# The opening of a two-layer convolution and GEGLU kernel: order of its first stage, filter tiles by sums and differences, and pair additions on GpSimd

## The chip, the core and the metric

The kernel runs on one core of a Trainium2 chip. The metric is the device time of one execution in microseconds (us). The core has a matrix engine (TensorE, PE in the profile; its weight loads are PEld), a vector engine (VectorE, DVE), a scalar engine (ScalarE, ACT), a general engine (GpSimd, POOL) and a queue engine (SyncE, SP). Each works through its own list of instructions in order. Matrix results land in PSUM, which GpSimd does not read here; everything else lies in SBUF.

## The reference

With S = 2048 tokens and D = 576 channels, four steps are applied to x = A_q:

```
x = x + A(layernorm(x));  x = x + B(layernorm(x));  x = x + A(layernorm(x));  x = x + B(layernorm(x))

A(q): kv = (k * shift_k summed over 4 taps along the sequence) * v
      y  = causal long convolution of kv with ssm_k over the sequence (by FFT) + kv * ssm_D
      return q * y
B(x): (gelu(x @ w_gate) * (x @ w_up)) @ w_down        w_gate, w_up: 576 x 4608
```

k, v and the filters do not depend on x, so y is computed once for both layers. Inputs and output are 16-bit.

## The kernel before

The sequence is cut into four chunks of 512 tokens, and a chunk into four row tiles of 128 partitions (`RT`). The convolution of a chunk is a short discrete transform by matrix products with cosine and sine tables (`W`, `Wx`): the filter chunk gives four frequency tiles `h0[kt]`, the kv chunk gives `kc[kt]`, each with a cosine and a sine part (s = 0, 1) of 576 columns. Their complex products (`kacc`, which calls `prod`, L365: a product of 1152 elements and an addition of 576, twice) go through the inverse tables into four output tiles Y0 to Y3 of the chunk.

Most of the run is the feed-forward part: gate/up matmuls (`gu`, L1570 for the first unit, L1650 later) and down matmuls (`dn`, L1684). A planner (`fill`, with the model times `t.pe`, `t.dve`, `t.act` and the costs `C_...`) threads the convolution of the later chunks between them. `quarter` (L247) makes such work units for the planner.

The change lies in the opening, which comes before the first gate/up matmul and whose order is written out by hand in `begin` (L833). The steps it issues are:

- The taps of the first kv chunk. The tap weights reach the partitions by small matmuls (L891, L899), and ScalarE copies them to `sx` (L901). The first 384 channels go through TensorE with diagonal matrices `dg` (L896) and transposed k (`kT`, `shift_taps`, L820); the last 192 channels go through VectorE (`taps_rest`, L945 to L953). Products with v end both (`taps_v`, L943; L953). Meanwhile GpSimd copies the tap weights for later chunks to `skc` (L912).
- The transposed filter chunk `hT0` (`turn_h`, L955; `copy_h`, L968).
- The filter tiles. Tiles 0 and 2 and half of 1 and 3 come from `pair_h`: `fwd_eo` (L235) puts the sum over even rows and the sum over odd rows side by side in PSUM, ScalarE copies both, and `cross` (L361) makes sum and difference on VectorE. The other halves of tiles 1 and 3 come from all four rows (`h_part`, `fwd_full`, L213). kv tiles come from `kfwd`.
- The products `kacc` for kt = 0, 2, 1, 3, and additions of tiles kt and kt + 2 (`pair0`, L1002, on VectorE at L1005), of which Y1 and Y3 need the differences (`pair0(0, 1)`, `pair0(1, 1)`); Y0 and Y2 are formed from the products directly (`straight`). The sums (`pair0(0, 0)`, `pair0(1, 0)`) are for later chunks.
- Row statistics of x: sums on ScalarE (`act_sum0`, L1187), squares on ScalarE (L1202), small steps `nm`, `ve`, `rstd` on GpSimd (L1194, L1209, L1210).
- The tail. Tile 0: `gate0` (L1457; its first step L1464 has Y in PSUM as an input, its second, L1467, two tiles in SBUF), `mean0`, `sq0`, `std0`, then `norm0` (L1414: reciprocal, normalisation L1420, a 64-wide copy L1422), `turn0` (transposes, L1436) and `copy0` (L1443) to `xnT`. Tile 2 likewise. Between them stand Y1 and Y3 (L417) and the copies of Y to SBUF (`keep_y`, L423).

Then `first_half` (L1506) starts the gate/up matmuls on tiles 0 and 2, while tiles 1 and 3 are gated and normalised.

PSUM tiles are drawn in turn from a pool of three (`ps` pool, tag "pr") and one of its own (`cps`). A tile that is drawn again waits until its last reader has finished. GpSimd's queue also issues the stores of `h0` and `kc` to memory and the loads of k and v for chunk 1.

Of the kernel before, what the change touches and what calls it, by code (L numbers as in the profile page):

```python
# [85 lines left out]
class Conv:  # L86
# [148 lines left out]
    def fwd_eo(self, src, kt, s, h, scale=1.0):  # L235

        nc = self.nc
        ps = self.ps()
        for e in range(2):
            for i in (e, e + 2):  # L240
                nc.tensor.matmul(ps[:, e, 0:HW], lhsT=self.fwd_w(kt, s, i),
                                 rhs=src[:, i, h * HW:(h + 1) * HW], start=(i == e), stop=(i == e + 2))
        eo, slot = self.eo_tile("eo")
        nc.scalar.activation(out=eo[:], in_=ps[:, :, 0:HW], func=ACT.Copy, scale=scale)
        return eo, slot

    def quarter(self, src, out, h, ready, seen, done, lent=False):  # L247
# [11 lines left out]
        def even():  # L259
            for kt, op in ((0, add), (2, sub)):  # L260
                tt(out=out()[kt][:, :, cols], in0=A[2][:], in1=A[3][:], op=op)
            when = t.on_dve(2 * C_R4)
            free[2](when), free[3](when)
            done(0, h, when + LAG)

        def odd():
            for kt, ops in ((1, (add, sub)), (3, (sub, add))):
                for s in range(2):
                    tt(out=out()[kt][:, s, cols], in0=A[0][:, s, :], in1=A[1][:, 1 - s, :], op=ops[s])
            when = t.on_dve(4 * C_BF)  # L270
            free[0](when), free[1](when)
            done(1, h, when + LAG)
# [9 lines left out]
        def one(n):  # L282
            def run():
# [76 lines left out]

    def cross(self, eo, lo, hi):  # L361
        for dst, op in ((lo, ALU.add), (hi, ALU.subtract)):
            self.nc.vector.tensor_tensor(out=dst, in0=eo[:, 0, :], in1=eo[:, 1, :], op=op)
# [469 lines left out]
    def begin(self, head, tables):  # L833
# [4 lines left out]
        with ExitStack() as es:  # L838
# [43 lines left out]
            idle = self.ps()  # L882

            def busy(n):
                for _ in range(n):
                    nc.tensor.matmul(idle[:, 0, 0:256], lhsT=full[:, 0:P], rhs=full, start=True, stop=True)  # L886
            busy(8)
            ps = self.ps()
# [5 lines left out]
            for db in range(nt):  # L894
                for j in range(KS):
                    nc.vector.tensor_scalar(out=dg[:, db, j, :], in0=self.ident[:], scalar1=wcol[:, db, j:j + 1], scalar2=None, op0=ALU.mult)  # L896
            ps = self.ps()
            for e, (lo, hi) in enumerate(((0, P), (P, DW))):
                nc.tensor.matmul(ps[:, e, 0:(hi - lo) * KS], lhsT=ones[:], rhs=sk1[:, nt * P + lo:nt * P + hi, :].rearrange("p d j -> p (d j)"),  # L899
                                 start=True, stop=True)  # L900
                nc.scalar.copy(out=sx[:, :, lo:hi], in_=ps[:, e, 0:(hi - lo) * KS].rearrange("p (d j) -> p j d", j=KS))  # L901
            busy(3)
            at = DW * KS - 512
            for db in range(nd + 1):
                nc.tensor.matmul(ps[0:width(db), 1, at + db:at + db + 1], lhsT=dvec[:, db * P:db * P + width(db)], rhs=ones[:, 0:1],
                                 start=True, stop=True)
            nc.scalar.copy(out=dcol[:, 0:nd], in_=ps[:, 1, at:at + nd])
            nc.scalar.copy(out=dcol[0:D - nd * P, nd:nd + 1], in_=ps[0:D - nd * P, 1, at + nd:at + nd + 1])
            for lo, hi, w in ((0, nd, P), (nd, nd + 1, D - nd * P)):
                nc.gpsimd.tensor_tensor(out=hn[0][0:w, lo:hi, 0], in0=hn[0][0:w, lo:hi, 0], in1=dcol[0:w, lo:hi], op=ALU.add)  # L910
            for j in range(KS):
                nc.gpsimd.tensor_copy(out=self.skc[0:1, j, :], in_=sk1[:, :, j])  # L912
            skT = tc.dram_tile([1, KS * D], BF16, name="skT")
            nc.gpsimd.dma_start(out=skT[:], in_=self.skc[0:1, :, :].rearrange("p j d -> p (j d)"))

            k, v = self.kt_[0], self.vt_[0]
            px = self.ps()
            for i in range(KS - 1):
                nc.tensor.matmul(px[:, i // 2, i % 2 * DW:(i % 2 + 1) * DW], lhsT=below[:], rhs=k[:, RT - KS + 1 + i, nt * P:D],
                                 start=True, stop=True)  # L920
            nc.scalar.copy(out=kx[:, 0:2, :], in_=px[:, 0, 0:2 * DW].rearrange("p (i c) -> p i c", c=DW))
            nc.scalar.copy(out=kx[:, 2, :], in_=px[:, 1, 0:DW])
            nc.vector.tensor_copy(out=kx[:, KS - 1:, :], in_=k[:, 0:RT, nt * P:D])
            DBS = [(0, 1), (2,)]
            for n, dbs in enumerate(DBS):
                pt = self.ps(True)
                for e, db in enumerate(dbs):
                    for u in range(RT):
                        nc.tensor.transpose(pt[:, e, u * P:(u + 1) * P], k[:, u, db * P:(db + 1) * P], self.ident[:])
                ne = len(dbs)  # L930
# [3 lines left out]
            def taps(dbs):  # L934
                out = self.ps()[:].rearrange("p e (i c) -> p e i c", i=RT)
                for e, db in enumerate(dbs):
                    self.shift_taps(k, kT, dg, P, db, out[:, e])
                return out

            def taps_v(dbs, out):  # L940
                ne = len(dbs)
                vd = v[:, :, dbs[0] * P:(dbs[0] + ne) * P].rearrange("p i (e c) -> p e i c", e=ne)
                nc.vector.tensor_tensor(out=vd, in0=out[:, 0:ne], in1=vd, op=ALU.mult)  # L943

            def taps_rest():  # L945

                cols, tt = slice(nt * P, D), nc.vector.tensor_tensor
                for j in range(KS - 1, -1, -1):
                    tt(out=wx[j < KS - 1][:], in0=kx[:, KS - 1 - j:KS - 1 - j + RT, :],  # L949
                       in1=sx[:, j, :].unsqueeze(1).to_broadcast([P, RT, DW]), op=ALU.mult)  # L950
                    if j < KS - 1:
                        tt(out=wx[0][:], in0=wx[0][:], in1=wx[1][:], op=ALU.add)  # L952
                tt(out=v[:, :, cols], in0=wx[0][:], in1=v[:, :, cols], op=ALU.mult)  # L953

            def turn_h(b):  # L955

                hv = hn[b][:].rearrange("p b (q i) -> p b i q", i=RT)
                pt = [self.ps(True) for g in range(2)]
# [7 lines left out]
            def copy_h(hT, pt):  # L966
                for g in range(2):
                    nc.scalar.copy(out=hT[:, 2 * g:2 * g + 2, :], in_=pt[g][:, :, 0:D])  # L968

            h0, kc, A = {}, {}, {}  # L970

            def h_part(b, kt, s, copy=None, ps=None, later=False):
                if b == 1:
                    t, src = self.H1[:, kt, :, :], self.hT1
                else:
                    t, src = h0[kt], hT0
                run = self.fwd_full(src, kt, s, t, copy, ps, later)
                if s == 1 and b == 0:
                    self.flush(0.0)
                    self.spill(self.Hd[b][kt], t)  # L980
                return run

            def straight(mt, kts):

                return [(self.inv_w(mt, s, mt == 2 and kt % 2 == 1), A[(s, kt)]) for kt in kts for s in range(2)]

            def kfwd(kt):
                kc[kt] = self.kcp.tile([P, 2, D], BF16, tag="kc", name="kc")
                for s in range(2):
                    self.fwd_full(v, kt, s, kc[kt])  # L990
                self.flush(0.0)
                self.spill(self.Kd[0][kt], kc[kt])
# [16 lines left out]
            def inv0(mt, ps):  # L1009
                self.inverse(0, mt, self.terms(mt, self.yb), ps)  # L1010
                return ps
            self.H1 = head.stay()

            def pair_h(kt, s, h):

                eo, slot = self.fwd_eo(hT0, kt, s, h)
                self.eo_free[slot] = 0.0
                cols = slice(h * HW, (h + 1) * HW)
                return lambda: self.cross(eo, h0[kt][:, s, cols], h0[kt + 2][:, s, cols])

            for kt in range(RT):
                pool, tag = (self.hrp, "hr") if kt == 0 else (self.krp, "kr")
                h0[kt] = pool.tile([P, 2, D], BF16, tag=tag, name="h0")
            pt = turn_h(0)
            taps_rest()
            ps = [taps(dbs) for dbs in DBS]
            copy_h(hT0, pt)
            for dbs, out in zip(DBS, ps):
                taps_v(dbs, out)
# [745 lines left out]
```

## Time and profile before

| what | us |
|---|---|
| runs shown: median (lowest to highest) | 914.1 (913.17 to 914.59) |
| the profiled execution | 914.25 |
| its span, first to last instruction | 912.5 |
| TensorE busy | 903.1 (99% of the span) |
| VectorE busy | 577.4 (63%) |
| ScalarE busy | 333.0 (36%) |
| GpSimd busy | 160.0 (18%) |
| first gate/up matmul starts | 39.67 |
| TensorE busy before it | 33.72 |
| VectorE busy before it | 32.18 |

A row of a timeline gives the start and the length in us, the engine, the line, the operation, the tiles written and read, the shapes and the count; in brackets stands the idle time before it and what ended it. A row of the groups gives busy time, mean length in ns and idle time. A chain of waits lists, in order of time, what the end waited for. Lengths of neighbours on one engine overlap by up to 0.1 us, so the distance of two starts is the price of an operation in a row of them. Time before 39.67 us is the opening.

### The profile page before, as it was taken

The numbers are of one execution on the slowest core, as the hardware profiler recorded it, in microseconds if no ns is written. First come the engines' busy times: TensorE is split into PE (matmuls) and PEld (weight loads), VectorE is DVE, ScalarE is ACT, GpSimd is POOL, SyncE is SP. The second block draws the span as 40 slices with busy tenths as digits, with TensorE's granted clock in tenths as the row PEclk, the third lists the DMA queues.
The fourth block names the chain that finished last, engine by engine and source line by source line (L and its number), as shares of the span: only waits on it lengthen the run. The fifth ranks groups of instructions, "written<-read, shape, count | busy, mean of one in ns | idle before, by whom it ended". The sixth has DMA issues, their size and how long they took to land.

```text
span 912.5 us, 19232 instructions
## 1 busy us (share of the span) xinstructions
PE 903.1 (99%) x8166; PEld 525.6 (58%) x8166; DVE 577.4 (63%) x985; ACT 333.0 (36%) x626; POOL 160.0 (18%) x333
## 2 busy tenths in 40 slices
PE   8899999999999999999999999999999999999998
PEld 6786556466465565664655655646646546556555
DVE  7889986679889876787898855442333335333332
ACT  6865545523323245353124133551121224321211
POOL 3403404220114031330204002220000003100000
PEclk9999999999999999999999999999999999999999
DMA  9979997849529509784925801981720721977720
GB/s 261 315 200 268 265 253 117 220 132 181 169 75 202 174 3 173 216 156 104 274 64 128 186 3 34 172 160 23 134 78 4 154 79 27 170 173 176 137 61 27
DMA packets 128955, 131.15 MB, mean 144 GB/s; under 512 B 43618, under 2 KB 120675, under 8 KB 128868
## 3 DMA queue, kind: packets, MB, share of 16 engines
q1 hardware_dynamic: 119232, 93.47, 49.0%
q0 software_dynamic: 9632, 36.43, 12.4%
q8 instruction: 64, 1.05, 0.5%
q14 instruction: 23, 0.19, 0.1%
q10 hardware_dynamic: 4, 0.01, 0.0%
HBM read 108.35 MB, written 11.80 MB: 132 GB/s over the span
## 4 chain that ended last, share of the span: by engine, by line
PE 98%; DVE 1%; ACT 0%; issue 0%; DVEq 0%
PE gu L1650 59%; PE dn L1684 31%; PE gu L1570 3%; PE cps L293 1%; PE ps L417 1%; PE ps L218 1%; PE cps L417 1%; PE ps L293 0%; DVE wx L949 0%; PE xps L1436 0%; PE cps L886 0%; DVE wx L952 0%; PE cps L218 0%; DVE x_c L1467 0%; DVE x_c L1464 0%; PE ps L963 0%
## 5 line engine op out<-in xcount | busy, mean ns | idle before, releaser
L1650 PE MATMUL gu<-xnT,wgu 64*128 64x512 bf16 x4968 | 540.7, 377 | 0.0
L1650 PEld LDWEIGHTS <-wgu 64*128 64x128 bf16 x4968 | 240.3, 94 | 293.7 <-issue 5.9
L1659 ACT ACTIVATE ga<-gu 128x512 f32<-128x512 f32 x258 | 153.8, 596 | 448.6 <-PE gu L1650 440.3
L1660 DVE TENSOR_TENSOR hT<-ga,gu 128x512 bf16<-128x512 f32 x258 | 177.1, 687 | 200.3 <-ACT ga L1659 199.0
L1684 PE MATMUL dn<-wd,hT 128*128 128x288 bf16 x2304 | 292.3, 287 | 0.0
L1684 PEld LDWEIGHTS <-hT 128*128 128x128 bf16 x2304 | 223.1, 98 | 65.9 <-issue 9.5
L1720 DVE TENSOR_TENSOR x_c<-x_c,dn 128x576 f32<-128x576 f32 x64 | 48.2, 753 | 56.4 <-PE dn L1684 56.1
L1194 POOL TENSOR_SCALAR nm<-s 128x1 f32<-128x1 f32 x60 | 20.3, 339 | 267.1 <-DVE x_c L1715 206.1
L1202 ACT ACTIVATE junk<-x_c,nm 128x576 bf16<-128x576 f32 x48 | 36.9, 769 | 29.1 <-POOL nm L1194 27.6
L1210 POOL TENSOR_TENSOR rstd<-ve,neghalf_t 128x1 f32<-128x1 f32 x62 | 41.5, 670 | 5.2
L557 POOL DMA_DIRECT2D hr<-Hd x32 | 17.4, 546 | 126.7 <-DVE prod L376 124.9
L1209 POOL TENSOR_SCALAR ve<-ss 128x1 f32<-128x1 f32 x62 | 25.4, 409 | 56.1 <-ACT junk L1202 56.0
L296 ACT COPY eo<-cps 128x576 f32<-128x576 f32 x31 | 19.8, 639 | 29.5 <-PE cps L293 20.0
L1266 ACT ACTIVATE xn<-x_c,nb,rstd 128x576 bf16<-128x576 f32 (+1 forms) x48 | 28.6, 644 | 5.1 <-POOL nb L1214 5.0
L1706 DVE TENSOR_TENSOR ob<-x_c,dn 128x576 bf16<-128x576 f32 x15 | 11.3, 754 | 29.0 <-PE dn L1684 25.8
L1549 ACT ACTIVATE ga<-gu 128x512 bf16<-128x512 f32 x26 | 15.5, 597 | 31.8 <-PE gu L1650 24.9
L1570 PE MATMUL gu<-xnT,wgu 64*128 64x256 bf16 x432 | 24.6, 270 | 0.0
L377 DVE TENSOR_TENSOR prod<-prod 128x576 bf16<-128x576 bf16 x48 | 22.0, 458 | 1.7
L1570 PEld LDWEIGHTS <-wgu 64*128 64x128 bf16 x432 | 20.6, 94 | 3.7 <-issue 0.9
L432 POOL DMA_DIRECT2D out_dram<-ob x12 | 6.8, 563 | 90.9 <-DVE ob L1706 70.7
L256 DVE SCALAR_TENSOR_TENSOR eo<-eo 128x576 f32<-128x576 f32 x22 | 16.4, 754 | 5.5 <-ACT eo L296 5.4
L617 DVE TENSOR_TENSOR zs<-sum,prod 128x576 f32<-128x576 bf16 x24 | 18.1, 755 | 0.5
(164 smaller groups left out, 582.4 us busy)
## 6 DMA issues: line engine op xcount, KB each, us to landing
wgu<-in_B_w_gate_dram SPq DMA_DIRECT2D x45, 576.0 KB, 6.2
wd<-in_B_w_down_dram SPq DMA_DIRECT2D x30, 864.0 KB, 7.8
wgu<-in_B_w_up_dram SPq DMA_DIRECT2D x45, 512.0 KB, 8.0
hr<-Hd POOLq DMA_DIRECT2D x32, 288.0 KB, 5.0
kr<-Kd POOLq DMA_DIRECT2D x24, 288.0 KB, 5.5
Kd<-kc POOLq DMA_DIRECT2D x12, 288.0 KB, 7.1
k<-in_A_k_dram POOLq DMA_DIRECT2D x3, 1008.0 KB, 13.2
wgu<-in_B_w_up_dram SPq DMA_DIRECT2D x45, 64.0 KB, 8.0
```

The source lines that it names most:

```text
L377: nc.vector.tensor_tensor(out=dst, in0=pr[:, 0, :], in1=pr[:, 1, :], op=ALU.subtract if part == 0 else ALU.add)
L1194: nc.gpsimd.tensor_scalar(out=v["nm"][:], in0=v["s"][:], scalar1=-1.0 / D, scalar2=None, op0=ALU.mult)
L1202: nc.scalar.activation(out=junk[:], in_=get_x(), func=ACT.Square, bias=v["nm"][:, 0:1], accum_out=v["ss"][:])
L1209: nc.gpsimd.tensor_scalar(out=ve[:], in0=v["ss"][:], scalar1=1.0 / D, scalar2=EPS, op0=ALU.mult, op1=ALU.add)
L1210: nc.gpsimd.tensor_tensor(out=v["rstd"][:], in0=ve[:], in1=neghalf_t[:, 0:1], op=ALU.pow)
L1266: nc.scalar.activation(out=xn[:, lo:hi], in_=x_c[c][:, j, 0:hi - lo], func=ACT.Identity, scale=v["rstd"][:, 0:1], bias=v["nb"][:, 0:1])
L1570: nc.tensor.matmul(pair[:, s, e * 256:(e + 1) * 256], lhsT=w[r0:r0 + HK, k, gi * P:(gi + 1) * P], rhs=xnT[r0:r0 + HK, blk_of[k], tok], sta ...
L1650: nc.tensor.matmul(pair[:, s, :], lhsT=w[r0:r0 + HK, k, gi * P:(gi + 1) * P], rhs=xnT[r0:r0 + HK, b, :], start=(k == 0), stop=(k == NKC - 1))
L1659: nc.scalar.activation(out=ga[:], in_=pair[:, 0, :], func=ACT.Gelu_apprx_tanh)
L1660: nc.vector.tensor_tensor(out=hT[:, fi, :], in0=ga[:], in1=pair[:, 1, :], op=ALU.mult)
L1684: nc.tensor.matmul(part[h][:, h, 0:HW], lhsT=hT[:, fi, at * P:(at + 1) * P], rhs=wd[2 * wb + fi // WT][:, fi % WT, h * HW:(h + 1) * HW], s ...
L1720: nc.vector.tensor_tensor(out=xh, in0=xh, in1=acc[:, :, 0:HW], op=ALU.add)
```

## The change

The opening is written anew; the work that it computes is the same.

- Of the taps, the weights' matmuls all stand ahead of ScalarE's copies. The VectorE part begins with the tap that needs no shifted rows, and the last four diagonals follow it. The transposes of k stand together. GpSimd's `skc` copies move behind the tap matmuls and behind a row sum.
- The filter tiles: `even` puts the sum over even rows of both column halves into a PSUM tile and copies it to SBUF as 32-bit data, `odd` adds the odd rows on top in the same PSUM tile and copies that as tile kt, and `apart` makes tile kt + 2 as twice the even sum minus the total (`differ`, VectorE, one input from PSUM). `fwd_eo`, `cross`, `pair_h` and `h_part` go.
- `pair0` runs on GpSimd, and both sums are issued in the opening.
- Row sums of tiles 0, 1 and 2 go to VectorE (`row_sum0`, a tensor reduction); tile 3's stays on ScalarE.
- Y1 and Y3 stand between the last products and `turn0`, with six matmuls and ten transposes that only keep TensorE at work. Both use the PSUM tile of its own. Y0 is copied to SBUF on VectorE.
- In `quarter`, `even` and `odd` are cut into single units, and the planner's pace in `first_half` changes.

```diff
-        self.nc.vector.scalar_tensor_tensor(out=self.halves(dst), in0=self.halves(eo[:]), scalar=2.0, in1=ps[:, :, 0:HW],
+        self.nc.vector.scalar_tensor_tensor(out=self.halves(dst), in0=eo[:], scalar=2.0, in1=ps[:, :, 0:HW],
                                             op0=ALU.mult, op1=ALU.subtract)
...
-                    self.U.append((at, 4 * C_BF, odd))
-                    self.U.append((at, 2 * C_R4, even))
+                    for kt, cost, run in ((1, 2 * C_BF, odd), (3, 2 * C_BF, odd), (0, C_R4, even), (2, C_R4, even)):
+                        self.U.append((at, cost, lambda kt=kt, run=run: run(kt)))
...
+            tt(out=wx[0][:], in0=k[:, 0:RT, rest], in1=tap(0), op=ALU.mult)
+            nc.vector.tensor_copy(out=kx[:, KS - 1:, :], in_=k[:, 0:RT, rest])
+            diagonals(nt - 1)
+            for j in range(1, KS):
+                tt(out=wx[1][:], in0=kx[:, KS - 1 - j:KS - 1 - j + RT, :], in1=tap(j), op=ALU.mult)
+                tt(out=wx[0][:], in0=wx[0][:], in1=wx[1][:], op=ALU.add)
+            tt(out=v[:, :, rest], in0=wx[0][:], in1=v[:, :, rest], op=ALU.mult)
...
+            head.act_sum(3)
+            for j in range(KS):
+                nc.gpsimd.tensor_copy(out=self.skc[0:1, j, :], in_=sk1[:, :, j])
...
+            def even(kt, s):
+                eo, slot = self.eo_tile("eo")
+                self.eo_free[slot] = 0.0
+                E[kt, s] = new(), eo
+                self.fwd_sum(E[kt, s][0], hT0, kt, s, 0)
+                nc.scalar.copy(out=eo[:], in_=E[kt, s][0][:, :, 0:HW])
+
+            def odd(kt, s):
+                ps, eo = E[kt, s]
+                self.fwd_sum(ps, hT0, kt, s, 1)
+                nc.scalar.copy(out=self.halves(h0[kt][:, s, :]), in_=ps[:, :, 0:HW])
+
+            def apart(kt):
                 for s in range(2):
+                    ps, eo = E[kt, s]
+                    self.differ(h0[kt + 2][:, s, :], eo, ps)
...
-            def pair0(kt, sg, parts=(0, 1)):
-                for part in parts:
+            def pair0(kt, sg):
+                for part in range(2):
                     b = self.ybp.tile([P, D], BF16, tag="yb", name="yb")
-                    nc.vector.tensor_tensor(out=b[:], in0=A[(part, kt)][:], in1=A[(part, kt + 2)][:],
+                    nc.gpsimd.tensor_tensor(out=b[:], in0=A[(part, kt)][:], in1=A[(part, kt + 2)][:],
...
+            even(0, 0)
+            even(0, 1)
+            kfwd(0, 0, small())
+            odd(0, 0)
+            odd(0, 1)
+            kfwd(0, 1, new())
+            head.row_sum(0)
+            head.row_sum(2)
+            apart(0)
+            head.row_sum(1)
+            head.act_sq(0)
             kacc(0)
+            put(0, h0, kc)
+            put(2, h0)
...
+            kfwd(2, 0, small())
+            kfwd(2, 1, new())
+            even(1, 0)
+            even(1, 1)
             kacc(2)
+            put(2, kc)
+            kfwd(1, 0, small())
+            odd(1, 0)
+            odd(1, 1)
+            kfwd(1, 1, new())
+            pair0(0, 1)
+            apart(1)
+            kacc(1)
+            put(1, h0, kc)
+            put(3, h0)
+            kfwd(3, 0, small())
             head.act_sq(2)
+            kfwd(3, 1, new())
             self.load_v(1, nc.gpsimd)
...
+            straight(0, (0, 2), True)
+            straight(2, (0, 2), True)
+            straight(0, (1,))
             kacc(3)
...
+            straight(0, (3,), last=True)
+            straight(2, (1, 3), last=True)
+            pair0(1, 1)
             head.act_sq(1)
             head.act_sq(3)
             head.gate(0, Y[0])
             head.mean(0)
+            put(3, kc)
             head.sq(0)
             head.std(0)
+            Y[1] = small()
+            busy(Y[1], 6)
+            self.inverse(0, 1, self.terms(1, self.yb), Y[1])
+            head.idle(10)
             head.gate(2, Y[2])
             head.mean(2)
+            self.keep_y(0, 1, Y[1])
             head.sq(2)
             head.std(2)
+            Y[3] = small()
+            self.inverse(0, 3, self.terms(3, self.yb), Y[3])
             head.norm(0)
+            head.turn(0)
+            nc.vector.tensor_copy(out=self.halves(self.y[0][:, 0, :]), in_=Y[0][:, :, 0:HW])
+            self.keep_y(0, 3, Y[3])
             head.norm(2)
             head.copy(0, nc.scalar.copy, nc.vector.tensor_copy)
+            head.turn(2, small_t())
+            head.copy(2, nc.scalar.copy, nc.vector.tensor_copy)
+            self.keep_y(0, 2, Y[2])
             nc.scalar.activation(out=warm[:], in_=head.zero, func=ACT.Gelu_apprx_tanh)
+            pair0(0, 0)
+            pair0(1, 0)
             head.gate(1, None, 0)
-            pair0(0, 0)
-            self.after = lambda: pair0(1, 0)
...
+        def row_sum0(j):
+            v = gvars[0][j]
+            v["s"] = small.tile([P, 1], F32, tag="s", name="s")
+            nc.vector.tensor_reduce(out=v["s"][:], in_=x_b[0][:, j, :], axis=mybir.AxisListType.X, op=ALU.add)
+            mean_after(v, 0.0)
             conv.steps.pop()[2]()
...
-                        t.dve, t.act = t.pe + 1.6, t.pe + 0.6
+                        t.dve, t.act = t.pe + 0.8, t.pe + 0.6
```

More of the change, by code (lines that the diff above doesn't have):

```diff
@@ L257, in apart, with even, odd, end @@
             t.on_dve(C_R4)
[L259 to L272, printed above, removed]
+        def even(kt):
+            tt(out=out()[kt][:, :, cols], in0=A[2][:], in1=A[3][:], op=sub if kt else add)
+            end(0, kt, t.on_dve(C_R4))
+        def odd(kt):
+            for s in range(2):
+                tt(out=out()[kt][:, s, cols], in0=A[0][:, s, :], in1=A[1][:, 1 - s, :], op=add if (kt == 3) == (s == 1) else sub)
+            end(1, kt, t.on_dve(2 * C_BF))
+        def end(e, kt, when):
+            if kt > 1:
+                for i in ((2, 3), (0, 1))[e]:
+                    free[i](when)
+                done(e, h, when + LAG)
         todo, going = [(0, 2), (1, 3)], []
@@ L880, in begin, with busy @@
             head.more(1)
[L882 to L884 removed]
+            new = lambda: self.psp.tile([P, 2, 512], F32, tag="pr", name="ps")
+            small = lambda: self.cpsp.tile([P, 2, 512], F32, tag="cps", name="cps")
+            new_t = lambda: self.psp.tile([P, 2, 1024], BF16, tag="pr", name="pt")
+            small_t = lambda: self.cpsp.tile([P, 2, 1024], BF16, tag="cps", name="cpt")
+            def busy(ps, n):
                 for _ in range(n):
[L886 to L888 removed]
+                    nc.tensor.matmul(ps[:, 0, 0:256], lhsT=full[:, 0:P], rhs=full, start=True, stop=True)
+            idle = small()
+            busy(idle, 8)
+            ps = new()
             for db in range(nt):
@@ L964, in turn_h, with copy_h @@
                 return pt
-            def copy_h(hT, pt):
-                for g in range(2):
+            def copy_h(hT, pt, order):
+                for g in order:
                     nc.scalar.copy(out=hT[:, 2 * g:2 * g + 2, :], in_=pt[g][:, :, 0:D])
[L970 to L988, printed above, removed]
-                for s in range(2):
-                    self.fwd_full(v, kt, s, kc[kt])
+            copy_h(hT0, turn_h(0), (0, 1))
+            out = []
+            for n, dbs in enumerate(DBS):
+                o = (new() if n else small())[:].rearrange("p e (i c) -> p e i c", i=RT)
+                for e, db in enumerate(dbs):
+                    self.shift_taps(k, kT, dg, P, db, o[:, e])
+                out.append(o)
@@ L1423, in norm0, with reserve0, idle0, turn0 @@
             xn0[j] = xn
-        def turn0(j, idle=0, two=False):
+        def reserve0(j, other=None):
+            pt = psp.tile([P, 2, 1024], BF16, tag="pr", name="xps")
+            turned[j] = [pt, pt if other is None else other]
+        def idle0(n):
+            for _ in range(n):
+                nc.tensor.transpose(turned[0][0][:, 0, 7 * P:8 * P], ident[:], ident[:])
+        def turn0(j, other=None):
             if 0 not in xnT_of:
                 xnT_of[0] = xtp.tile([P, NKC, CH], BF16, tag="xnT", name="xnT")
-            new = lambda: psp.tile([P, 2, 1024], BF16, tag="pr", name="xps")
-            pt = [new()]
-            pt.append(new() if two else pt[0])
-            turned[j] = pt
-            for _ in range(idle):
-                nc.tensor.transpose(pt[0][:, 0, 7 * P:8 * P], ident[:], ident[:])
+            if j not in turned:
+                reserve0(j, other)
+            pt = turned[j]
             for b in range(NKC):
```

155 lines of the change are left out of this document (48 added, 107 removed).

## The prediction

> **What bounds the kernel now.** First the stretches (microseconds; busy time of TensorE, its weight loads, VectorE, ScalarE, GpSimd; granted clock; DMA share; GB/s), then the chain of waits.
>
> ```profile
> 32.18:34.87 2.69, 0.00 (x1) 0.00 (x1) 2.48 (x8) 2.41 (x6) 1.86 (x4) 1.00 1.03 402
> 34.87:36.00 1.13, 1.13 (x15) 1.00 (x16) 1.09 (x5) 1.10 (x5) 0.00 (x0) 1.00 1.04 413
> 36.00:39.40 3.40, 3.40 (x22) 2.37 (x19) 1.74 (x5) 1.99 (x4) 0.00 (x0) 0.51 0.99 367
> ...
> 39.67:67.00 27.33, 27.33 (x464) 22.62 (x465) 24.36 (x45) 17.96 (x35) 4.13 (x7) 1.00 0.73 201
> 67.00:905.00 838.00, 838.00 (x7389) 474.50 (x7388) 519.15 (x858) 285.27 (x535) 138.26 (x290) 1.00 0.60 135
> ```
>
> From 39.67 us on, where the first gate/up matmul starts, TensorE never waits, at full clock. So the end follows one number, that start, which I call G. The profiled execution took 914.25 us (span 912.5 and 1.75 around it; the median of the runs shown is 914.1), and the new time is 914.25 + (G − 39.67). The reordered units in `quarter` and the pace 0.8 in `first_half` only shuffle VectorE later; TensorE's unbroken 865 us cover that, and I cost it at nothing. If a convolution matmul came to wait there, it would cost that wait.
>
> Before G, the chain runs through VectorE: tap products up to 15.18, filter tiles and products up to 29.68, then gates and norms, and at last through TensorE:
>
> ```profile
> 34.82 0.05 issue
> 34.87 0.68 PE xps L1436 x9
> 35.55 1.33 PE cps L417 x8
> 36.88 0.96 PE xps L1436 x9
> 37.83 1.83 PE ps L417 x8
> 39.67 6.00 PE gu L1570 x108
> ```
>
> The two groups of eight (Y1, Y3) stand in the way at about half clock: eight such matmuls took 0.98 at full clock (0.49 for four in L218).
>
> **Taps.** Row L949 took 1.07 and 0.94 us beside GpSimd's copies L912, and 0.56 after them:
>
> ```profile
> 8.05 1.07 DVE L949 TENSOR_TENSOR wx<-kx,sx 128x768 bf16<-128x768 bf16 x1
> ...
> 8.65 2.02 POOL L912 COPY skc<-sk 1x576 bf16<-1x576 bf16 x2
> ...
> 10.14 0.94 DVE L949 TENSOR_TENSOR wx<-kx,sx 128x768 bf16<-128x768 bf16 x1
> ...
> 11.12 0.56 DVE L952 TENSOR_TENSOR wx<-wx,wx 128x768 bf16<-128x768 bf16 x1
> ```
>
> The change puts these copies behind a row sum on ScalarE, about 12.4 to 15, and takes the 0.67 us wait of L899 on ScalarE away. ScalarE's tap rows are then ready at about 5.7. VectorE: start 5.9 (was 7.56), first product 0.56, copy 0.35, four diagonals at 0.17, seven operations at 0.56: 11.4. Then the two products from PSUM, 1.15 + 0.65 (L943): 13.3 instead of 15.18. TensorE's tap matmuls end at 12.15 as before, so they don't delay it.
>
> **Filter tiles.** Twelve `cross` operations go (3.03 + 1.56 = 4.59 us); four `differ` come at 0.75 (L256, the same operation from SBUF; L1464, with one PSUM input, 0.81): 3.0. Three row sums on VectorE replace three on ScalarE. No row shows a tensor reduction; the bounds are 0.41 (L1005, 16-bit) and 0.755 (L1720, one result per element from 32-bit data). I take 0.7, nearest the 32-bit row, since one sum per row can't be written in pairs; two of the three lie in a wait anyway. After 13.3 TensorE does eight kv matmuls and four odd ones (1.47, and 0.16 to the last one's end), ScalarE copies (0.65), so `differ` starts at 15.6, with two hand-overs of 0.05 at 15.7. Then 2 × 0.75, the third sum 0.7, two product groups `kacc` at 2.33 (18.45 to 20.78), two `differ`, two `kacc`: 15.7 + 1.5 + 0.7 + 4.66 + 1.5 + 4.66 = 28.7; with 0.1 for the last one's end and 0.1 of hand-overs, 28.9. Before, this end, E, was 29.68. The eight saved filter matmuls (0.98) lie under VectorE. ScalarE loses three sums (0.66 each) off the path.
>
> **Tail without collisions.** E to the first normalised tile is 5.35 us in both: the gate needs Y0's last four matmuls (0.65), for which the two pair additions (0.76) were a cover. So taking those off VectorE gains nothing there. Between the two norms a 0.75 copy of Y0 takes the place of two pair additions (0.74): the second tile at E + 7.0 in both. Then the change gains: instead of 3.0 us of half-clock matmuls only five transposes, 0.3, their end 0.2, and a copy of 0.68 (L1443): about 1.3. G = 28.9 + 7.0 + 1.3 = 37.2. Alone this gives 914.25 − 2.45 = 911.8.
>
> **The pair additions in GpSimd.** This is the disputed price. Eight additions of 128x576 leave VectorE (0.41 each). No row has such an addition on GpSimd. The nearest rows are the copies of 576 elements:
>
> ```profile
> L912 POOL COPY skc<-sk x4: 675/1028/1042, 7.0 to 9.6; 1x576 bf16<-1x576 bf16 x4
> ```
>
> Undisturbed 0.675; next to VectorE 1.03, of which 0.57 after VectorE's operation ended. Bounds for an addition, T: 0.57, as if the second input were free, and 2 × 0.675 = 1.35. I take two readings of 0.57 and the 0.1 around them, 1.25. In a sentence of its own: the Trainium skill, GPSIMD Engine Reference, 3.1 Elementwise — side-by-side cycle accounting, gives 4497 ns for an addition of 2048 elements, so an estimate of 1.26 for 576, and the sum would come out 0.04 higher.
>
> What matters more is that the two engines exclude each other. In the rows above each waits for the whole of the other's operation. Small ones show for which operands:
>
> ```profile
> 31.27 0.82 DVE L1467 SCALAR_TENSOR_TENSOR x_c<-x_c,rstd,x_b 128x576 f32<-128x576 f32 x1
> 31.45 0.69 POOL L1209 TENSOR_SCALAR ve<-ss 128x1 f32<-128x1 f32 x1 [0.54 <-ACT junk L1202]
> ```
>
> ```profile
> 32.20 0.80 DVE L1464 SCALAR_TENSOR_TENSOR x_c<-x_b,nm,ps 128x576 f32<-128x576 bf16 x1
> ...
> 32.78 0.18 POOL L1209 TENSOR_SCALAR ve<-ss 128x1 f32<-128x1 f32 x1
> ```
>
> Beside two SBUF inputs `ve` takes 0.69 and ends 0.05 after VectorE; beside one PSUM input 0.18. So `differ` and the gate's first step are free, but `kacc`, the gate's second step and probably the norms are not. Placing the additions:
> - Pair (0,1) is queued behind six DMA issues of 0.58 and the first tile's `ve` and `rstd`; GpSimd comes to it at about 23.6, when the `differ` pair has 0.5 left. The next product waits T − 0.45, then the second addition slips in and the next add waits T − 0.05: 2T − 0.5 = 2.0 us on E.
> - Pair (1,1) stands behind a filter store that waits for an earlier one's landing (issued about 20, 9.1 us to landing) and for `ve`, `rstd`, a v load. It runs into the first gate's second step: T − 0.5 = 0.75. Y1 waits for it on TensorE, and behind Y1 stand the idle transposes and Y3; on ScalarE behind Y1's copy the second square and root, which have about 1 us of slack.
> - Of the last four, issued as soon as GpSimd is free, one meets the second norm or its copy: T − 0.1 = 1.15. Where two meet it, another T.
>
> Together 4T − 1.05 = 3.95, G = 41.15, time 915.7. Ends: T = 0.57 gives 913.0, T = 1.35 gives 916.1.
>
> **The clock.** Before, 1.13 us of work in the 3.4 us up to 36.0 was followed by 3.4 us at half clock, costing 1.66. With the collisions TensorE has some 1.9 us idle, 0.5 of transposes and 0.55 idle before G; whether a window falls so depends on its phase. I add half, 0.8: **916.5**. (By the Trainium skill, TensorE: Matmul & The Clock Gate, Part 1, the clock falls after a whole idle window of 3413 ns; by that rule nothing would be added and the time is 915.7. Here a third of the window was busy and it fell all the same.)
>
> **The rivals.**
> 1. *The exclusion costs nothing*: the additions find VectorE on PSUM inputs, or hold the port for a fraction of their time. For it: the first pair was put just ahead of the two `differ`, which don't exclude it. Against: the L912 and L1467 rows. Decides: 4T − 1.05 under 0.5, so an effective T under 0.4. Then G = 37.2, **911.8**, faster; if only Y1's lateness counts, through ScalarE's queue, G about 38.6, 913.2.
> 2. *Half of it*: the kv products collide, the tail doesn't, because GpSimd is late and its last four fall behind the norms: 37.2 + 2.0 + 0.3 for Y1, G = 39.5, **914.1**, no change.
> 3. *The saving doesn't arrive, whatever the additions cost*: the 9 to 13 us landings hold pair (1,1) until after 34, Y1's copy holds ScalarE, and G reaches 43.5: **918.1**. For it: DMA share over 1.0 up to 39. Against: the same transfers landed in time before. It is the upper part of my own case.
>
> **How the numbers follow.** Collisions about as priced, with or without the clock: 0.55 (third rival in it), 915.0 to 918.5. Half: 0.17. None: 0.28. Of 914.1, 0.2% is 1.8 us, about what a measurement can tell from no change; faster is below 912.4, slower above 916.0. Faster: 0.28 and little of the half case, 0.29. Slower: 0.55 less the mild part, 0.50. Same: 0.21. The range takes in most of the first rival (911.8 to 913.2) and leaves out its lower edge and the worst landings: 911.6 to 918.3.
>
> **What would show it.** Tap products done by 13.3; a GpSimd addition row of about 1.25; `kacc` product or add rows beside it near 2 us instead of 0.755 and 0.46; a norm row far over 0.58 or its 64-wide copy over 1 us; G near 41 with a window of half clock. If additions take 1.25 and no VectorE row beside them grows, the exclusion was misread; if G comes at 37 to 38, the first rival holds. I would be wrong by placement if the additions run, but beside PSUM operations.

## The result and the profile after

The kernel after takes **921.17 us** (median of 4 runs, 920.48 to 921.59) where the kernel before takes 913.63 in the same session (4 runs, 913.1 to 914.59): a ratio of 1.0081, 95% interval 1.0063 to 1.0098. The profiled execution took 921.34, its span 919.5. That is slower, as forecast, but between the profiled executions by 7.1 us instead of 2.3 (by 7.5 between the medians), and outside the range. Executions of the kernel before fall into two groups, 913.08 to 913.85 at a mean granted clock of 0.999 to 1.0 and 914.13 to 915.33 at 0.997 to 0.998, so a time that is set against a start G, which is read in a profile, is that of the profiled execution (914.25 before, at 0.998).

The first gate/up matmul, G, starts at 45.56 us (39.67 before). In the chain of waits the longest piece ahead of it is one VectorE instruction, the second step of the gate for tile 2:

```profile
35.98 5.87 DVE x_c L1481 x2
...
45.56 7.43 PE gu L1583 x108
```

The stretches (TensorE, its weight loads, VectorE, ScalarE, GpSimd, granted clock, DMA share, GB/s) show what comes of it:

```profile
35.00:38.40 3.40, 3.40 (x21) 2.30 (x19) 3.29 (x3) 1.31 (x4) 3.29 (x5) 0.54 1.04 413
45.60:48.00 2.40, 2.40 (x24) 1.93 (x25) 2.26 (x5) 2.37 (x4) 0.00 (x0) 0.50 0.00 0
60.00:900.00 840.00, 840.00 (x7524) 477.74 (x7522) 527.21 (x872) 292.22 (x547) 135.50 (x290) 1.00 0.60 137
```

From G on TensorE is still never idle for long, so the end still follows G. But the gate/up matmuls now begin at half clock: the first 108 took 7.43 us, 6.00 before. So the 7.1 us are 5.89 of G and 1.43 of that, less 0.2 elsewhere.

The early part went as planned or better. VectorE's timeline, from the second tap product on:

```profile
12.14 0.68 DVE L965 TENSOR_TENSOR v<-ps,v 128x512 bf16<-128x512 f32 x1
12.74 1.40 DVE L1460 TENSOR_REDUCE s<-x_b 128x1 f32<-128x576 bf16 x2
15.26 1.42 DVE L232 SCALAR_TENSOR_TENSOR h<-eo,ps 128x576 bf16<-128x576 f32 x2 [1.13 <-ACT h L983]
```

Tap products end at 12.8, `differ` starts at 15.26, with 0.71 each.

What went otherwise stands in the next two views of the kernel after: GpSimd's timeline, then VectorE's.

```profile
24.03 0.55 POOL L411 DMA_DIRECT2D Kd<-kc  x1
24.60 2.52 POOL L1010 TENSOR_TENSOR yb<-yb 128x576 bf16<-128x576 bf16 x2
...
30.15 0.62 POOL L180 DMA_DIRECT2D v<-in_A_v_dram  x1
30.80 1.28 POOL L1010 TENSOR_TENSOR yb<-yb 128x576 bf16<-128x576 bf16 x1
...
35.60 0.63 POOL L411 DMA_DIRECT2D Kd<-kc  x1
36.26 4.95 POOL L1010 TENSOR_TENSOR yb<-yb 128x576 bf16<-128x576 bf16 x4
```

```profile
24.04 3.40 DVE L361 TENSOR_TENSOR yb<-prod 128x576 bf16<-128x576 bf16 x1
...
30.46 1.94 DVE L361 TENSOR_TENSOR yb<-prod 128x576 bf16<-128x576 bf16 x1
...
35.98 5.85 DVE L1481 SCALAR_TENSOR_TENSOR x_c<-x_c,rstd,x_b 128x576 f32<-128x576 f32 x1
```

Undisturbed these three rows take 0.46, 0.46 and 0.82. Each is held until GpSimd has finished not one addition but **all that stand in a row**: the first ends 0.32 after the pair of 24.60 to 27.12, the third 0.62 after the four of 36.26 to 41.21. The second met one addition alone, since the next waited for this row's own `yb`. The excess is 2.94 + 1.48 + 5.03 = 9.45 us, all on the path; 45.56 less 9.45 is 36.1.

### The profile page after: what moved, and what is told of

Same layout as the page of the kernel before. It is cut to its first block, busy times and chain, and to the rows that moved or that the text cites. A ratio compares the mean times of both kernels' runs of the same rounds, so it can differ in the third digit from the quotient of the medians.

```text
span 919.5 us, 19224 instructions
## 1 busy us (share of the span) xinstructions
PE 906.3 (99%) x8167; PEld 527.4 (57%) x8167; DVE 584.0 (64%) x973; ACT 331.0 (36%) x619; POOL 165.8 (18%) x341
## 3 DMA queue, kind: packets, MB, share of 16 engines
q8 instruction: 64, 1.05, 0.5%
## 4 chain that ended last, share of the span: by engine, by line
PE 95%; DVE 4%; ACT 0%; issue 0%; DVEq 0%
PE gu L1663 59%; PE dn L1697 31%; PE gu L1583 3%; PE cps L281 1%; DVE yb L361 1%; DVE x_c L1481 1%; PE ps L401 1%; PE cps L401 0%; PE ps L281 0%; DVE h L232 0%; DVE prod L360 0%; DVE prod L358 0%; PE cps L873 0%; DVE v L965 0%; DVE wx L933 0%; DVE wx L932 0%
## 5 line engine op out<-in xcount | busy, mean ns | idle before, releaser
L1211 POOL TENSOR_SCALAR ve<-ss 128x1 f32<-128x1 f32 x62 | 22.9, 369 | 53.6 <-ACT junk L1204 53.5
L1246 DVE SCALAR_TENSOR_TENSOR x_c<-g_t,rstd,x_c 128x576 f32<-128x576 f32 x16 | 13.0, 813 | 8.6 <-POOL rstd L1212 8.6
```

Source lines behind the costliest of these rows:

```text
L1211: nc.gpsimd.tensor_scalar(out=ve[:], in0=v["ss"][:], scalar1=1.0 / D, scalar2=EPS, op0=ALU.mult, op1=ALU.add)
```

## The experiments

Theories. *Whole runs*: VectorE waits for an unbroken run of GpSimd additions, and that is the loss. *One at a time*: what I had predicted, the engines alternate. *Rewriting*: the new order itself, with its waits, costs the time, whatever the additions do. All ratios are to the kernel before, run on the same chip; kernel 1 is the kernel of experiment 1, and so on. Where a diff leaves lines out, `...` stands for them.

**1. All pair additions back on VectorE** (the last four also where they had stood before).

```diff
-            def pair0(kt, sg):
+            def pair0(kt, sg, eng=nc.vector):
-                    nc.gpsimd.tensor_tensor(out=b[:], in0=A[(part, kt)][:], in1=A[(part, kt + 2)][:],
+                    eng.tensor_tensor(out=b[:], in0=A[(part, kt)][:], in1=A[(part, kt + 2)][:],
...
```

> The changed kernel with all eight pair additions back on VectorE (the last four placed as in the kernel before). Theory R: the whole loss is that VectorE operations with two SBUF inputs wait for whole runs of GpSimd additions (three rows of 3.40, 1.94 and 5.85 us hold 9.45 us above their undisturbed length). Then the first gate/up matmul comes at 45.56 - 9.45 plus 0.8 for the first pair on VectorE, about 36.9, and the time is 911.5 to 913 us, below the kernel before. Rival W, the rewriting itself costs (tiles, waits, clock): the time stays above 916.

Measured: 912.07 us (911.77 to 912.79), ratio 0.9981 [0.9972, 0.9989]; G = 36.99, no row held. TensorE's timeline has one new wait:

```profile
49.42 4.11 PE L1584 MATMUL gu<-xnT,wgu 64*128 64x256 bf16 x72 [0.51 <-DVE hT L1590]
```

The rewriting is faster than the kernel before (its slowest run, 912.79, is below every run of that), so that theory falls: the additions on GpSimd cost some 9 us.

**2. Only the last four back on VectorE.**

```diff
-            def pair0(kt, sg):
+            def pair0(kt, sg, eng=nc.gpsimd):
...
-            pair0(0, 0)
-            pair0(1, 0)
             head.gate(1, None, 0)
+            pair0(0, 0, nc.vector)
+            self.after = lambda: pair0(1, 0, nc.vector)
```

> The changed kernel with only the last four additions back on VectorE, where the kernel before had them; the pairs (0,1) and (1,1) stay on GpSimd. Theory R: the 5.85 us row falls to 0.8, the rows of 3.40 and 1.94 stay: first gate/up matmul at about 40.5, time 915 to 916.5. One-at-a-time theory of the prediction: the last four cost only about 1.2 us, so the time stays near 920.

Measured: 916.71 (914.97 to 917.46; the profiled one 915.33), ratio 1.0029 [1.002, 1.0039]; G = 40.16. Two runs of two are left, 2.52 and 2.50 long, and hold an add (2.90 instead of 0.46) and the first gate's second step (2.66 instead of 0.82). So the run of four cost 5.4 of G: the loss goes with the length of the run. The second hold, GpSimd and VectorE:

```profile
30.80 0.62 POOL L180 DMA_DIRECT2D v<-in_A_v_dram  x1
31.45 2.50 POOL L1010 TENSOR_TENSOR yb<-yb 128x576 bf16<-128x576 bf16 x2
```

```profile
31.92 2.66 DVE L1481 SCALAR_TENSOR_TENSOR x_c<-x_c,rstd,x_b 128x576 f32<-128x576 f32 x1
```

This row began 0.47 after the first addition and still waited for both.

**3. The kernel before, with its pair additions on GpSimd and nothing else changed.**

```diff
-                    nc.vector.tensor_tensor(out=b[:], in0=A[(part, kt)][:], in1=A[(part, kt + 2)][:],
+                    nc.gpsimd.tensor_tensor(out=b[:], in0=A[(part, kt)][:], in1=A[(part, kt + 2)][:],
```

> The kernel before with nothing changed but the engine of the pair additions, GpSimd instead of VectorE, at the same places of the program. They come to GpSimd behind the statistics at about 33.6 us, six of them nearly in a row. Theory R: the first norm waits for the run, some 7 us, and the time is 920 to 924. One at a time: norm, its copy and the second norm wait 1.2 us each, 917 to 918.5. Rival W: near 914.

Measured: 923.68 (922.75 to 924.21), ratio 1.0107 [1.0093, 1.0121]; G = 48.25. GpSimd's timeline and VectorE's:

```profile
36.97 0.62 POOL L427 DMA_DIRECT2D Kd<-kc  x1
37.61 7.40 POOL L1005 TENSOR_TENSOR yb<-yb 128x576 bf16<-128x576 bf16 x6
```

```profile
34.74 1.15 DVE L1420 TENSOR_SCALAR xn<-x_c,nm,rstd 128x576 bf16<-128x576 f32 x1
...
37.16 8.17 DVE L1420 TENSOR_SCALAR xn<-x_c,nm,rstd 128x576 bf16<-128x576 f32 x1
```

Here both behaviours stand side by side: the first norm (0.58 alone) met a run of two and waited for one addition, the next a run of six and waited for all. The run of two follows a small `rstd` step on GpSimd, the run of six a DMA issue; that difference is what the next kernels try. They differ also in when the norm began, inside the first addition or ahead of it, but kernel 2's row began inside it and was held.

**4. to 6. Additions and copies whose results nothing uses, in the kernel before.** In each kernel three stand beside the `kacc` of kt = 2 and three behind the issue of the v load. Kernel 4 has copies of 128x576 behind the small `nm`, then one-partition additions. Kernel 5 has additions of 128x576 behind `nm`, then additions with a memset behind each. Kernel 6 has the additions right behind the issue of a `Kd` spill, then without memsets. The edit in kernel 5:

```diff
+            for i in range(3):
+                nc.gpsimd.tensor_tensor(out=probe[i][:, :], in0=hT0[:, 0, :], in1=hT0[:, 1, :], op=ALU.add)
             kacc(2)
...
             self.load_v(1, nc.gpsimd)
             head.act_sum(1)
+            for i in range(3):
+                nc.gpsimd.tensor_tensor(out=probe[i][:, :], in0=hT0[:, 0, :], in1=hT0[:, 1, :], op=ALU.add)
+                nc.gpsimd.memset(mark[i][:], 0.0)
```

> The kernel before with six extra GpSimd operations on scratch tiles that nothing reads: three copies of 128x576 (one input) beside the products of kt = 2, and three additions of 1x576 (two inputs, one partition) beside those of kt = 3. If runs hold VectorE whenever all 128 partitions take part, one product or add row beside the copies grows by a whole run, about 2 us, and the one-partition additions alternate with VectorE, about 1.2 us on each of several rows. If runs hold VectorE whenever the GpSimd operation has two inputs, the copies alternate (rows of about 1.0 instead of 0.755 and 0.46) and one row beside the additions grows by about 3.7 us.

> Before, with three extra GpSimd additions (128x576, 16 bits) beside the third kacc, behind a small GpSimd instruction (nm) and not behind a DMA issue, and three more behind the issue of load_v, each followed by a GpSimd memset of 128x1. Their results are used by nothing. Theory 'whole runs': a VectorE instruction that comes during the first three waits for all of them, one row longer by 2.4 to 3.8 us, as in the kernel after. Theory 'whole runs, but only behind a DMA issue': the first three alternate with VectorE, rows longer by 0.3 to 1.2 each, as with the first two additions of the six in the experiment on the kernel before. For the second three: if anything that reads no SBUF ends a run, several VectorE rows are longer by at most 1.3 each; if a run goes on over the memsets, one VectorE row is longer by 3.4 to 4.6. The time itself is not the question: between 913.5 and 922, since the square roots' small steps wait behind the additions.

> The counterpart: before, with three extra additions right behind the DMA issue of a Kd spill, beside the third kacc, and three behind the issue of load_v with nothing between them. Their results are used by nothing. Theory 'whole runs': both groups hold one VectorE row each for 2.4 to 3.8 us beyond its own time. Theory 'one at a time': no row longer by over 1.3 us. If the first group holds here and the one behind a small instruction does not, the DMA issue is what decides; if both hold, it is not. Time 913.5 to 922.

Kernel 4 (920.21 once): copies alternate, VectorE rows of 0.80, 1.21, 0.80 (0.46, 0.75, 0.46 alone); the one-partition additions too, 1.25 for 0.82. At these places the forms of kernel 4 don't hold VectorE for a run. Kernel 5 (922.44 once), behind the small instruction, GpSimd and VectorE:

```profile
22.62 4.96 POOL L1048 TENSOR_TENSOR probe<-hT 128x576 bf16<-128x576 bf16 x3
```

```profile
23.26 1.42 DVE L377 TENSOR_TENSOR yb<-prod 128x576 bf16<-128x576 bf16 x1
24.60 1.83 DVE L376 TENSOR_TENSOR prod<-kc,h 128x1152 bf16<-128x1152 bf16 x1
26.47 1.43 DVE L377 TENSOR_TENSOR yb<-prod 128x576 bf16<-128x576 bf16 x1
```

Kernel 6 (922.85 once), the same three additions behind the DMA issue:

```profile
22.09 0.55 POOL L427 DMA_DIRECT2D Kd<-kc  x1
22.66 3.74 POOL L1046 TENSOR_TENSOR probe<-hT 128x576 bf16<-128x576 bf16 x3
```

```profile
22.36 4.36 DVE L363 TENSOR_TENSOR h<-eo 128x288 bf16<-128x288 f32 x1
```

Behind `nm` VectorE gets in after each addition, every row 1.0 longer, and GpSimd waits too (1.65 an addition). Behind the issue one row of 0.45 takes 4.36, and GpSimd runs at 1.27 an addition. Kernel 6's second group holds a product for 5.36 (0.75 alone), kernel 5's with the memsets an addition for 5.14: memsets between the additions don't let VectorE in. In these three kernels small steps wait behind the additions on GpSimd, so their times tell nothing more.

**7. After, with a memset behind each pair addition.**

```diff
                                             op=ALU.subtract if sg else ALU.add)
+                    nc.gpsimd.memset(marks.pop()[:], 0.0)
```

> After, with a memset of 128x1 on GpSimd behind each of its eight pair additions; nothing else is changed. Theory 'whole runs' with a memset that ends a run: the row that was 5.85 falls to about 2.1 (0.82 + 1.25), the others of the tail pay 0.3 to 1.2 where they meet an addition, the first gate/up matmul starts between 41 and 43.5 instead of 45.56, and the time is 916 to 919 (my prediction's collisions come true). If a memset does not end a run: rows of 3.4 and 5.8 to 6.3, first gate/up matmul at 45.6 to 46.5, time 921 to 923.

Measured: 922.06 (920.77 to 922.17), ratio 1.0082 [1.0068, 1.0095], G = 45.55; held rows of 2.85, 2.69 and 5.36, the last a norm in the place of the gate. No memset ended a run.

**8. and 9. After, with a small instruction ahead of each pair of additions**: in 8 arithmetic that reads SBUF, in 9 a memset.

```diff
             def pair0(kt, sg):
+                nc.gpsimd.tensor_scalar(out=marks.pop()[:], in0=head.zero, scalar1=-1.0, scalar2=None, op0=ALU.mult)
```

> After, with one small GpSimd instruction (tensor_scalar, 128x1) ahead of each pair of additions, so that no run stands right behind a DMA issue. Theory 'a run behind a DMA issue holds VectorE, one behind a small instruction alternates': VectorE's rows are longer by at most 1.3 each, GpSimd's additions where they meet VectorE take 1.4 to 1.8 instead of 1.25, the first gate/up matmul starts between 39.5 and 43.5 instead of 45.56, the time is 915 to 919. Theory 'what decides is something else, for example whether VectorE was in the middle of an instruction': the row of 5.85 stays above 4, first gate/up matmul at 44.5 to 46, time 920 to 922.

> The same with a memset of 128x1, which reads nothing, in the place of the small arithmetic instruction. If any instruction between the DMA issue and the run is enough: as the kernel with the small instruction, 915 to 919. If it must be one that reads SBUF: as after, rows of 3.4 and 5.9, 920.5 to 922. Memsets between the additions of a run had not ended it (a row of 5.36), which speaks for the second.

Measured for 8: 917.25 (917.15 to 917.93), ratio 1.0032 [1.0021, 1.0044]. Its GpSimd, VectorE and TensorE:

```profile
25.21 0.22 POOL L1009 TENSOR_SCALAR mark<-neghalf_t 128x1 f32<-128x1 f32 x1
25.41 3.17 POOL L1012 TENSOR_TENSOR yb<-yb 128x576 bf16<-128x576 bf16 x2
```

```profile
25.62 1.82 DVE L358 TENSOR_TENSOR prod<-kc,h 128x1152 bf16<-128x1152 bf16 x1
27.48 1.41 DVE L361 TENSOR_TENSOR yb<-prod 128x576 bf16<-128x576 bf16 x1
...
38.31 0.16 DVE L1423 RECIPROCAL rstd<-std 128x1 f32<-128x1 f32 x1 [1.67 <-ACT std L1500]
38.51 1.22 DVE L1424 TENSOR_SCALAR xn<-x_c,nm,rstd 128x576 bf16<-128x576 f32 x1
39.77 1.13 DVE L1426 COPY xn<-xn 128x64 bf16<-128x64 bf16 x1
```

```profile
41.97 6.07 PE L1585 MATMUL gu<-xnT,wgu 64*128 64x256 bf16 x108 [0.56 <-DMA wgu<-in_B_w_up_dram]
```

VectorE's rows beside the additions are 0.1 to 1.1 longer, none more. G comes right behind ScalarE's last copy to `xnT`, which ends at 41.91, whatever the bracket names. Four instructions of 0.2 to 0.7 us that compute nothing of use take back about 4 us of the 7.5 that the change had lost. Measured for 9: 921.3 (920.97 to 922.14), ratio 1.0073 [1.0056, 1.009], held rows 3.35, 1.97 and 5.92: as after. So what stands between the DMA issue and the run decides: small arithmetic that reads SBUF breaks the hold, a memset does not. The memset is also shorter (0.12 against 0.21 to 0.66), and no kernel here tells which difference counts.

**10. The other forms behind a DMA issue**: the kernel before, one-partition additions at kernel 6's first place, copies at its second.

```diff
             kfwd(2)
+            for i in range(3):
+                nc.gpsimd.tensor_tensor(out=probe[i][0:1, :], in0=hT0[0:1, 0, :], in1=hT0[0:1, 1, :], op=ALU.add)
...
             self.load_v(1, nc.gpsimd)
+            for i in range(3):
+                nc.gpsimd.tensor_copy(out=probe[i][:, :], in_=hT0[:, 0, :])
```

> Before, with three additions of 1x576 (one partition) right behind the issue of a Kd spill, and three one-input copies of 128x576 right behind the issue of load_v; results used by nothing. It tells whether the form of the instruction or the place behind the DMA issue decides. If the place alone decides: one VectorE row longer by about 3.5 in each group (additions of 128x576 at these two places gave 3.9 and 4.6). If only two-input additions on 128 partitions hold: no row longer by over 1.3 in either group. Time 913.5 to 922.

Measured (919.38 once), the groups by tile (min/median/max ns):

```profile
L1046 POOL TENSOR_TENSOR probe<-hT x3: 1280/1477/1767, 22.4 to 25.4; 1x576 bf16<-1x576 bf16 x3
L1058 POOL COPY probe<-hT x3: 668/675/911, 33.6 to 34.8; 128x576 bf16<-128x576 bf16 x3
```

The one-partition additions alternate (VectorE rows 1.83, 1.41, 1.82) at the place where those on 128 partitions held. One addition of VectorE waited for two of the three copies (1.75 instead of 0.45), and the third copy then waited for VectorE. So of the forms tried here only the two-input additions on 128 partitions held VectorE to the run's end, and they only at this place; the copies lie between, neither theory's case.

**11. Kernel 1 with the planner's pace of before.**

```diff
-                        t.dve, t.act = t.pe + 0.8, t.pe + 0.6
+                        t.dve, t.act = t.pe + 1.6, t.pe + 0.6
```

> After with all pair additions on VectorE (912.07 on record) and the planner's clock of VectorE in first_half set back from t.pe + 0.8 to t.pe + 1.6, as before. If the 0.51 us wait of the gate/up matmuls for hT at 49.4 us comes from the earlier planned conversion work, it goes, and the time is 911.5 to 911.7. If the wait only moves, the time is within 0.2 of 912.07.

Measured: **911.58** (911.38 to 912.45), ratio 0.9972 [0.9962, 0.9982], G = 36.74: the fastest kernel here. The wait of 0.51 is gone from the trace. The interval overlaps that of kernel 1, and 0.25 of the gain is a G that the pace can't move, so the time alone doesn't show the pace's worth.

**12. Kernel 11 with the first four additions on GpSimd, behind a small instruction.** The edit is that of kernel 8 in `pair0`, for these four alone.

> The fastest kernel so far (after with all pair additions on VectorE and the pace of 1.6: 911.58), with the first four additions back on GpSimd, each pair behind a small arithmetic instruction so that they alternate with VectorE. Question: does GpSimd's help pay at all once whole runs are gone? 'It pays': VectorE saves four rows of 0.41 and meets collisions that fall where it waits anyway, first gate/up matmul at 36.3 to 36.7, time 911.0 to 911.5. 'It does not': as with the small instruction ahead of all eight, two rows beside the kacc products are longer by about 1.0 each and the matmuls of Y1 and Y3 wait for additions that end 1.5 to 2 us later, first gate/up matmul at 38.0 to 39.5 (36.74 without), time 912.8 to 914.5.

Measured: 915.9 (915.36 to 916.67), ratio 1.0017 [1.0008, 1.0026], G = 41.25, later than either theory said. Beside the lengthened rows (1.41, 1.82, 1.14) TensorE waits 2.88 us for pair (1,1), which GpSimd ends at 35.5, and Y3 behind it takes 2.13 at half clock (1.14 in kernel 11); ScalarE's copy of Y1 delays the second root and the second norm by 1.53. Even without long runs GpSimd's help doesn't pay here.

## Why the prediction was right or wrong

- **Bound.** Right: the end followed G in every kernel, to within 0.6 us plus the clock.
- **Taps, filter tiles.** Right, a little too dear: 12.83 instead of 13.3, `differ` at 15.26 instead of 15.7, 0.71 instead of 0.75 each; the reductions are 0.7 apart as taken.
- **Opening without collisions.** 1.1 too dear: 37.2 forecast, 45.56 less 9.45 is 36.1. E has 0.9 of it (32.40 less the 4.42 held there is 28.0, forecast 28.9); the tail behind E was right to 0.2, 8.1 instead of 8.3. That kernels 1 and 11, with the additions on VectorE, come so near to 37.2 and 911.8 (G = 36.99 and 36.74, 912.07 and 911.58) is in part chance: there pair (0,1) stands in the chain with 0.74.
- **T = 1.25.** Right: rows of 1.26 to 1.29 in the kernel after, 1.24 apart. The estimate of 1.26 that I had worked out from the Trainium skill's 4497 ns for 2048 elements (GPSIMD Engine Reference, 3.1 Elementwise — side-by-side cycle accounting) agrees.
- **The collisions.** This is the step that failed: "The next product waits T − 0.45, then the second addition slips in", and with it 4T − 1.05 = 3.95. VectorE did not get in between two additions; it waited for whole runs, 9.45. Which operands matter was read rightly where it could be seen: a gate's first step, with one PSUM input, kept its 0.81 beside an addition (33.21, against 32.48 to 33.75). Kernel 8, where the engines do alternate, came to G = 41.97 and 917.25, near the 41.15 and 916.5 forecast, but partly by luck: from 36.1 it is 5.9, not 3.95. E pays 2.02 there, as priced, and the second gate's step 0.11; the two norms and a 64-wide copy pay 2.15, not 1.15, and 1.67 is VectorE waiting for the second root, which stands behind Y1's copy on ScalarE, where I had assumed 1 us of slack. My rows showed copies on one partition (L912) and 128x1 steps; one-partition additions alternate too (kernels 4 and 10). I noted "Where two meet it, another T" and gave it no weight. The places were off as well: the first gate's second step escaped, since that pair's second addition waited for its `yb`, and the second gate's met the run of four. The three terms add up to 4T − 1.1 = 3.9, not 4T − 1.05, and the taps to 13.2, not 13.3; neither decides anything.
- **What a page says.** The Trainium skill (SBUF — State Buffer, Who interferes with whom) gives the shared port pair to whichever engine issues its instruction first, for the whole of that instruction. The alternating rows agree (1.42 and 1.83 in kernel 5). The held ones don't: the row of 4.36 in kernel 6 started 0.30 before the first addition and yet waited for three, and the row of 2.66 in kernel 2 started inside the first of two and waited for both. Here the measurement decides.
- **The clock.** The term had the right sign and was too small: 0.8 forecast, 1.43 measured in the first 108 gate/up matmuls. It follows 2.67 us in which TensorE waited for the held norm, with waits of 0.89 and 0.56 and 1.1 of work behind it; kernel 8, where TensorE's longest wait behind Y3 is 0.77, has a row of 6.07, and kernel 7, with a wait of 3.32, one of 8.26. That these waits cause it is argued from the rows, not tested. By the Trainium skill (TensorE: Matmul & The Clock Gate, Part 1), whose rule asks for a whole idle window of 3413 ns, nothing would have been lost in the kernel after, since no wait ahead of its G is that long.
- **The rivals.** "Costs nothing" and "half" are out. "The saving doesn't arrive" was wrong in its mechanism: pair (1,1) was not held by a landing. A landing did hold GpSimd elsewhere, 2.28 us at 22.93 for `skT`, which I hadn't foreseen: `skc` was moved late and its broadcast load waits for it. Kernels 1 and 11, with the additions on VectorE, keep that order of the copies and are faster than before all the same.
- **The sum.** From 916.5 to 921.34: 5.5 more for the collisions, 0.6 more for the clock, 1.1 less for the opening without collisions, 0.2 less elsewhere.

## What to carry over

Before moving work to an engine that can keep a busy one waiting, measure a run of several such instructions in the form and the place meant, not one of another form: here the price of a collision was the run's length, not the instruction's. Look at what stands ahead of the run; a small instruction that reads SBUF between a DMA issue and the run brought back about half of the loss. And an addition that costs 0.41 on the bound engine was cheaper there than 1.25 beside it.

## What was not expected of the hardware

- Runs of 128x576 two-input additions on GpSimd right behind a DMA issue held a VectorE instruction with two SBUF inputs, or a norm, to the run's end: rows of 2.66 to 8.17 us in kernels 2 and 3, with two to six additions. Behind `nm`, `rstd` or a 128x1 `tensor_scalar` the engines alternated.
- Which engine began first did not decide. Some held rows began before the first addition (0.30 us in kernel 6, and 1.0 in its second group, 31.31 against 32.32), while GpSimd was issuing DMAs; others up to 0.48 into it (31.92 against 31.45 in kernel 2, 32.25 against 31.77 in kernel 7).
- Some held rows would have ended before the first addition: the product of 31.31 in kernel 6 by 32.06, against 32.32, and the add of 24.04 in the kernel after by 24.50, against 24.60. As far as GpSimd's rows can be trusted, a hold can thus begin during the issues. Issues alone held nothing: beside those from 27.05 to 28.70 in the kernel after, the rows took 0.74, 0.46 and 0.75. What holds VectorE, and why small arithmetic ends it, is open; a run with neither a DMA issue nor arithmetic ahead of it was not tried.
- One-partition additions of 576 take 1.28, as those on 128 partitions do (1.27).
- VectorE's reductions ran beside GpSimd's copies (11.67 to 14.29 in the kernel after) in 0.74 each, undisturbed, where the tap products before had taken 0.94 to 1.07.
